# A tuned attention-plus-feed-forward kernel: query weights loaded through transposing DMAs, key-value sums formed the other way round, and all steps in a new order

## The chip, the cores and the metric

The kernel runs on one core of one Trainium2 chip. The metric is the device time of one execution in microseconds (us); lower is better. Five engines work side by side: PE (TensorE, matmuls), DVE (VectorE), ACT (ScalarE), POOL (GpSimd) and SP (SyncE, which here only issues DMAs). Each takes its own instructions strictly in order. They wait for one another through semaphores.

## The reference

The input x has 2048 tokens of 448 features. It is normalised per token, and two branches are computed from the same normalised x and added to x: a linear attention with 16 heads of 28 features, and a feed-forward block of width 1792 with the mish activation. All inputs and the output are bf16.

```python
xn = _layernorm(x)
qkv = (xn @ wqkv)                                  # 448 -> 3 x 16 heads x 28
pq = einsum("bhsd,hdf->bhsf", q, w_phi);  pk = einsum("bhsd,hdf->bhsf", k, w_phi)
phi_q = concatenate([softmax(pq), softmax(-pq)]);  phi_k = concatenate([softmax(pk), softmax(-pk)])
kv = einsum("bhsf,bhsd->bhfd", phi_k, v);          z = sum over s of phi_k
o = einsum("bhqf,bhfd->bhqd", phi_q, kv) / (einsum("bhqf,bhf->bhq", phi_q, z) + 1e-6)
h = xn @ w1 + b1
out = x + o @ wo + (h * tanh(softplus(h))) @ w2
```

## The kernel before

The 2048 tokens are 16 tiles of 128, taken in 8 pairs u = 0 to 7. Everything stays in on-chip memory: x, both weight sets, the activations. The program is a list of named steps, `ORDER`, written out as text. Each name calls a function that records instructions for the engines; a small recorder (`Program`) notes which instruction reads and writes what and puts in the semaphore waits. So the order of the names sets the order of every engine's queue at once, and an instruction that must wait holds up all that stands behind it on its engine. SP's queue holds nearly all DMAs, loads and turns alike; the bias (`lba`) and W2 (`l2a`) are issued by ACT.

The steps, with the letters used in the order:

- `lx..`, `lkm`, `lqm`, `lvm`, `lkt`, `lqt`, `lp`, `l1m`, `l1t`, `l2`, `lo`: loads of x (in parts), of the key, query and value weights (rows 0 to 383, and the last 64 rows twice as a tail), of w_phi, W1, W2 and Wo. The last letter is the issuing engine (s is SP, a is ACT).
- `st`, `rs`, `xn`, `xt`: layernorm statistics of a pair (DVE), reciprocal deviation (ACT or POOL), the normalised pair (DVE or POOL), and its transpose into `xnT`, either by PE with a copy (letters a, d) or by one DMA (m, line 465).
- `wtk`, `wtq` and `wmk`, `wmq`: w_phi is folded into the key and query weights. The weights are transposed on PE (`w_tr`, line 493), copied out, and multiplied with a block-diagonal w_phi (`w_mm`, line 506). This gives `Wpk` and `Wpq`. Query weights so take 16 transposes and two copies.
- `kUF`, `kUH`, `vUF`, `vUH`, `qQ.GF`, `qQ.GH`, `fQ.CF`, `fQ.CH`: products with xnT, all at line 393 (`pair_part`). F is the part over three full blocks of 128 rows, six matmuls for two tiles; H is the rest of 64 rows, two matmuls, one in each half of the array. When both parts are done ACT applies exp (k, q) or mish (f), or ACT or DVE copies (v). q and f work on 1024 tokens at a time (half Q = 0 or 1), f on one of 14 blocks C of the hidden width.
- `knU.S`: k's softmax. DVE sums the exponentials and takes the reciprocal, POOL multiplies (line 551).
- `kvU`: the sums over tokens of phi_k times [v, 1], accumulated in one bank (line 570). Per pair 32 matmuls: for each sign s, tile, head group g and half r, a stationary 128x56 block of phi_k and 58 moving columns of v. The two halves r write different partitions.
- `kvz`: DVE masks the sums into `KVZ`, with the epsilon (lines 582 and 587).
- `ndT`: numerator and denominator of a tile T: 16 matmuls of 60 columns (line 641), then seven DVE instructions. The result goes through a DMA transpose (`otUm`, line 676) to `wo`.
- `gT`, `woUF`, `woUH`: second feed-forward product (14 matmuls, line 710) and output projection (line 725), accumulated in one bank per tile. After the third part DVE adds x, and `sto` or `stt` stores.
- `zN`: N warm-up matmuls on zeros. `b1` turns the bias. `pi`, `pm`, `pw`, `pk`, `pv`: masks, identity, zeros and ones made on POOL. `table` loads ACT's exp table.

PSUM has eight banks, which the recorder hands out in pairs to open products. A step that needs a pair waits until the engine that empties it is done.

Of the kernel before, what the change touches and what calls it, by code (L numbers as in the profile page):

```python
# [12 lines left out]
D = 448  # L13
# [15 lines left out]
KVW = 2 * (DH + 1)  # L29
# [119 lines left out]
pk lx1s lba zero pm lx2s st1 z12 pw lkms pi table st3 rs3a rs1p b1 lps xn1d bd wtk0a xn3p lkts lqms st2 z2 xt1a wtk1d  # L149
lqts wmk0a rs2p wtq0d wtq1d wmk1a pv xt3d wmq0a lx4s xn2p wmq1a lvms st7 st4 rs4p rs7a xn7d k1F k3F xn4p st5 lx0s st6  # L150
k1H rs5p v1Hd xt2m xt7m k3H v3Ha v1Fa v3Fa rs6a xn5d k2F v2Fd xn6p k2H v7Hd v2Ha xt4m xt5m k7H v7Fa k7F st0 rs0a v4Fa
kn1.1 k4F xt6m kn3.1 k5H v4Ha kn3.0 k4H v5Hd k5F xn0d v6Fa kn7.1 xt0m v5Fa q1.2F q1.2H kn2.0 kn5.0 k0H q1.1H v6Hd
kn2.1 k0F q1.1F v0Fa kn5.1 kn7.0 kn4.0 k6F k6H q0.1H v0Hd q1.3H q0.1F q1.3F q0.0F q1.0F kn4.1 q0.2H q1.0H l1ts kn6.0
kn6.1 q0.0H kv4 l1ms kv5 kv7 kv2 q0.2F los q0.3F f0.1F kn0.1 f1.8H q0.3H kn1.0 f0.1H kv1 kv3 kv6 kn0.0 kv0 f1.8F kvz
f1.10F f1.1F f1.5H f1.1H nd2 f1.10H f1.5F f0.0F f0.2H f1.11H f0.0H nd0 f0.2F f1.11F f1.7F f0.13F f1.7H f0.13H nd1
f1.13H f1.13F f1.9F f0.6F ot0m f0.6H nd3 f1.9H f0.8H f0.8F f0.5F f0.9F f0.5H f0.7H f0.9H nd4 f0.7F f1.2F nd5 ot1m
f1.12H f0.10H f1.2H l2a f0.10F f1.12F f1.3F f1.6H f0.12H f1.3H nd6 f1.6F f0.12F f0.11F f1.4H nd7 f0.4H f0.11H f0.4F
f1.4F f0.3F ot3m nd10 nd11 f0.3H ot2m f1.0H f1.0F wo3F g6 wo0F wo3H ot5m wo0H nd8 nd9 g1 g0 g7 wo5F nd14 ot4m nd12
wo2H wo5H g4 wo1F g5 g11 g10 wo2F wo4F nd13 wo1H wo4H sto3 nd15 ot6m g3 sto2 ot7m g9 g12 g2 wo6H wo7H g15 sto5 sto0
g8 g13 wo6F sto4 wo7F stt15 g14 sto1 sto6 stt14  # L160
# [8 lines left out]
def _kernel(es, nc, A_x, A_wqkv, A_w_phi, A_wo, B_w1, B_b1, B_w2, out):  # L169
# [10 lines left out]
    mask2 = sb("mask2", [P, 2], FP32)  # L180
# [18 lines left out]
    Wq = sb("Wq", [P, 4, D], BF16)  # L199
    Wqk = [Wq, Wk]  # L200
    Wp = [sb("Wpq", [P, 4, G * P], BF16), sb("Wpk", [P, 4, D], BF16)]
    WT = [[sb(f"WT{w}{i}", [GP, 2, G, P], BF16) for i in range(2)] for w in range(2)]
    actT = sb("actT", [P, FC, S], BF16)
    zeros = actT[:, 0, 0:TCW]
    Sk = [sb(f"Sk{i}", [P, 2, 2 * H], FP32) for i in range(NU)]
    rSk = [sb(f"rSk{i}", [P, 2, 2 * H], FP32) for i in range(NU)]
    v_flat = sb("v_all", [P, NU * 2 * H * (DH + 1)], BF16)
    v_all = v_flat[:, :].rearrange("p (u i h c) -> p u i h c", u=NU, i=2, h=H)
    EqT = sb("EqT", [P, 2, G, S], BF16)
    KVZ = sb("KVZ", [P, 2, G, 2, DH + 2], BF16)  # L210
# [15 lines left out]
    oT_home = [(Wkv, 0, ["Wk", "Wv"]), (Wkv, 14 * P, []), (Wq, 0, ["Wq"]), (Wp[1], 0, ["Wp1"])]  # L226
    home_rows = {"Wk": [("Wk", 0), ("Wt", 0), ("Wt", 1)], "Wv": [("Wv", 0)], "Wq": [("Wq", i) for i in range(3)],
# [65 lines left out]

    def p_ident():
# [19 lines left out]
    def p_ones():  # L314
        op("POOL", lambda e: e.memset(v_all[:, :, :, :, DH:DH + 1], 1.0), w=[("v1",)], tag="pv0")

    def p_mask2():
        op("POOL", lambda e: e.memset(mask2[:], 1.0), w=[("mask2",)], tag="pk0")
        for r in range(2):
            lo, hi = HALF[r]  # L320
            op("POOL", lambda e, lo=lo, hi=hi: e.affine_select(
                out=mask2[lo:hi], in_=mask2[lo:hi], compare_op=ALU.is_ge, fill=0.0, base=0, channel_multiplier=1,
                pattern=[[-DH, 2]]), r=[("mask2",)], w=[("mask2",)], tag="pk1")
            op("POOL", lambda e, lo=lo, hi=hi: e.affine_select(
                out=mask2[lo:hi], in_=mask2[lo:hi], compare_op=ALU.is_ge, fill=0.0, base=DH - 1, channel_multiplier=-1,
                pattern=[[DH, 2]]), r=[("mask2",)], w=[("mask2",)], tag="pk2")
        op("POOL", lambda e: e.tensor_copy(ap_on(KVZ[:, 0, 0, 0, DH + 1:DH + 2], [[NDW, 2 * G], [DH + 2, 2]]),
                                           ap_on(mask2[:, 0:1], [[0, 2 * G], [1, 2]])), r=[("mask2",)], w=[("KVZ1",)],
           tag="pk3")

    def zero():
        op("DVE", lambda e: e.memset(zeros.bitcast(mybir.dt.uint32), 0), w=[("zeros",)], tag="zeros")

    def warm(n):
        b = take1()

        def f(e):
            for _ in range(n):
                ins = e.matmul(bank(b)[:, :], zeros[:, 0:P], zeros[:, :], start=True, stop=True)
            return ins  # L340
        pe(f, [("zeros",)], [pb(b)], f"warm{n}")
# [142 lines left out]
    def w_tr(which, h, eng):  # L484
# [5 lines left out]
        def tr(e):  # L490
            for c in range(2):
                for g in range(G):
                    ins = e.transpose(oT()[:, c, g, :], Wqk[which][:, 2 * h + c, g * GP:(g + 1) * GP], ident[:])
            return ins
        pe(tr, rows_of("Wq" if which == 0 else "Wk")[:1 + 2 * h] + [("ident",)], [pb(b)], f"wtr{which}{h}")
        evac(eng, lambda: WT[which][h][:, :, :, :].rearrange("p c g n -> p (c g n)"),
             lambda: oT().rearrange("p c g n -> p (c g n)"), [pb(b)], [("WT", which, h)], f"wtre{which}{h}")

    def w_mm(which, h, eng):
        b = take2(False)  # L500
        n = (P, GP)[which]

        def mm(e):
            for c in range(2):
                for g in range(G):
                    ins = e.matmul(bank(b + c)[:, g * n:(g + 1) * n], WT[which][h][:, c, g, :], Wbd[:, g, :, 0:n // 2],
                                   start=True, stop=True)
            return ins
        pe(mm, [("WT", which, h), ("Wbd", 0), ("Wbd", 1)], [pb(b), pb(b + 1)], f"wmm{which}{h}")
# [47 lines left out]
    def kv_mm(u):  # L557
# [6 lines left out]
        def f(e):  # L564
            for s in range(2):
                for par in range(2):
                    for g in range(G):
                        for r in range(2):
                            at = (s * G + g) * KVW
                            ins = e.matmul(bank(kvb)[64 * r:64 * r + QP, at:at + KVW],  # L570
                                           E_of(u)[:, s, par, (4 * r + g) * QP:(4 * r + g + 1) * QP],
                                           v_all[:, u, par, 8 * r + 2 * g:8 * r + 2 * g + 2, :],
                                           start=(first and s == 0 and par == 0 and g == 0), stop=(last and par == 1),
                                           skip_group_check=True)
# [3 lines left out]
    def kvz():  # L578
        kvb = kv_bank[0]
        for r in range(2):  # L580
            lo, hi = 64 * r, 64 * r + QP
            op("DVE", lambda e, r=r, lo=lo, hi=hi: e.tensor_tensor(
                ap_on(KVZ[lo:hi, 0, 0, 0, 0:1], [[NDW, 2 * G], [DH + 2, 2], [1, DH]]),
                ap_on(bank(kvb)[lo:hi, 0:1], [[KVW, 2 * G], [DH + 1, 2], [1, DH]]),
                ap_on(mask2[lo:hi, 0:1], [[0, 2 * G], [1, 2], [0, DH]]), ALU.mult),
               r=[pb(kvb), ("mask2",)], w=[("KVZ", r)], tag=f"kvz{r}")
            op("DVE", lambda e, r=r, lo=lo, hi=hi: e.scalar_tensor_tensor(
                ap_on(KVZ[lo:hi, 0, 0, 0, DH:DH + 1], [[NDW, 2 * G], [DH + 2, 2]]),
                ap_on(bank(kvb)[lo:hi, DH:DH + 1], [[KVW, 2 * G], [DH + 1, 2]]), DEN_EPS / 2,
                ap_on(mask2[lo:hi, 0:1], [[0, 2 * G], [1, 2]]), ALU.add, ALU.mult),  # L590
               r=[pb(kvb), ("mask2",)], w=[("KVZz", r)], tag=f"kvzz{r}")
        free2(kvb)

# [39 lines left out]
    def nd(t):  # L633
        b = take2(False)

        def f(e):
            for s in range(2):
                for g in range(G):
                    for r in range(2):
                        at = (s * G + g) * NDW  # L640
                        ins = e.matmul(bank(b + r)[:, at:at + NDW], EqT[64 * r:64 * r + QP, s, g, tok(t)],  # L641
                                       KVZ[64 * r:64 * r + QP, s, g, :, :], start=True, stop=True)
            return ins
        pe(f, [("Eq", s, g, t // 8) for s in range(2) for g in range(G)]
           + [(n, r) for n in ("KVZ", "KVZz") for r in range(2)] + [("KVZ1",)], [pb(b), pb(b + 1)], f"nd{t}")
# [119 lines left out]
    for which, n in ((0, "q"), (1, "k")):  # L765
        for h in range(2):
            for eng, c in (("ACT", "a"), ("DVE", "d")):
                add(f"wt{n}{h}{c}", w_tr, which, h, eng)
# [10 lines left out]
    for eng, c in (("SP", "s"), ("ACT", "a")):  # L779
        for name, a, b in (("x0", 0, 2), ("x1", 2, 4), ("x2", 4, 8), ("x4", 8, 16)):  # L780
            add(f"l{name}{c}", load_x, a, b, eng)
        for i, (n, t) in enumerate((("q", Wq), ("k", Wk), ("v", Wv))):
            add(f"l{n}m{c}", load_main, eng, "W" + n, t, A_wqkv[:, i * D:(i + 1) * D])
        add(f"lqt{c}", load_tail, eng, "Wq", Wq, A_wqkv[:, 0:D])
# [3 lines left out]
        for name, fn in (("p", load_phi), ("b", load_b1), ("2", load_w2), ("o", load_wo)):  # L788
            add(f"l{name}{c}", fn, eng)
    add("b1", bias_T)  # L790
    for n, fn in (("pi", p_ident), ("pm", p_mask), ("pw", p_wbd), ("pv", p_ones), ("pk", p_mask2), ("zero", zero)):
        add(n, fn)
# [55 lines left out]
```

## Time and profile before

| what | value |
|---|---|
| median of 3 runs | 158.92 us (157.85 to 158.98) |
| profiled execution | 159.08 us, of which the span of instructions is 157.3 |
| PE busy, share of the span | 150.2 us, 95% |
| DVE | 100.6 us, 64% |
| ACT | 73.4 us, 47% |
| POOL | 42.0 us, 27% |
| moved by DMA | 12.72 MB |
| granted TensorE clock | 1.00 |

The span runs from the first to the last instruction, and the execution's own time is 1.8 us longer. In the profile a line such as "PE PS L393 MATMUL" names the engine, what it writes and the line of the kernel. PEld is the load of a matmul's stationary operand; it overlaps with PE. Rows of a timeline give start and duration in us; because matmuls are pipelined, each one's duration includes its latency, and the start of the next row tells when its columns had gone in. Waits are listed as who waited for whom: total us, times, longest. SPq is SP's issuing of a DMA; "us to landing" counts from the start of that.

### The profile page before, as it was taken

How to read it: one execution, taken by the hardware profiler on the slowest of the kernel's cores; microseconds unless marked ns; L12 is line 12 of the kernel's file. 1: busy time of each engine (PE TensorE's matmuls, PEld its weight loads, DVE VectorE, ACT ScalarE, POOL GpSimd, SP SyncE). 2: the span in 40 equal slices, each digit the busy share in tenths (PEclk: the TensorE clock that was granted, in tenths of full speed). 3: DMA queues.
4: the chain of work that ended last, by engine and by line, in shares of the span. 5: the costliest groups of instructions: out<-in, count | busy, mean ns of one | idle time of the engine just before them, and what ended most of it. 6: DMA issues, size and time to landing. Idle time of an engine off the chain costs nothing.

```text
span 157.3 us, 3093 instructions
## 1 busy us (share of the span) xinstructions
PE 150.2 (95%) x1309; PEld 74.1 (47%) x1309; DVE 100.6 (64%) x220; ACT 73.4 (47%) x84; POOL 42.0 (27%) x57
## 2 busy tenths in 40 slices
PE   6699999969999999999999999999999999999992
PEld 2394444424464644444444444555455555545550
DVE  2995899999994217745486665969686159710141
ACT  3286989969989768765578566300000000000000
POOL 6494767599999400000000000000000000000000
PEclk9999999999999999999999999999999999999999
DMA  4994353199400000003216604230310000940104
GB/s 155 284 329 107 71 105 70 23 212 367 130 10 0 4 0 4 0 0 58 41 21 194 214 4 79 38 63 2 58 58 4 0 0 0 154 142 0 58 26 149
DMA packets 20217, 12.72 MB, mean 81 GB/s; under 512 B 13932, under 2 KB 19436, under 8 KB 20204
## 3 DMA queue, kind: packets, MB, share of 16 engines
q1 hardware_dynamic: 18368, 10.92, 27.7%
q10 hardware_dynamic: 1836, 1.61, 3.4%
q8 instruction: 10, 0.16, 0.5%
q14 instruction: 3, 0.02, 0.1%
HBM read 7.48 MB, written 1.84 MB: 59 GB/s over the span
## 4 chain that ended last, share of the span: by engine, by line
PE 77%; DVE 10%; DMA 7%; SPq 3%; issue 1%; POOL 1%; DVEq 0%
PE PS L393 38%; PE PS L710 27%; PE PS L725 7%; DMA x_all<-in_A_x_dram 5%; DVE stats L412 3%; PE PS L641 3%; PE PS L570 2%; DVE xn L446 2%; DVE Sk L547 2%; DMA xnT<-xn 2%; SPq L265 1%; DVE mv L414 1%; SPq L260 1%; SPq L257 1%; DVE rSk L549 0%
## 5 line engine op out<-in xcount | busy, mean ns | idle before, releaser
L393 PE MATMUL PS<-xnT,W 128*128 128x512 bf16 (+1 forms) x224 | 45.8, 379 | 0.0
L710 PE MATMUL PS<-W,actT 128*128 128x448 bf16 x224 | 43.6, 353 | 0.0
L619 ACT ACTIVATE actT<-PS,b1T 128x1024 bf16<-128x1024 f32 x28 | 30.3, 1112 | 14.6 <-PE PS L393 14.6
L710 PEld LDWEIGHTS PS<-W,actT 128*128 128x128 bf16 x224 | 21.6, 98 | 20.6 <-issue 0.7
L393 PEld LDWEIGHTS PS<-xnT,W 128*128 128x128 bf16 (+1 forms) x224 | 17.6, 97 | 23.8 <-issue 4.3
L551 POOL TENSOR_TENSOR actT<-actT,rSk 128x896 bf16<-128x896 bf16 x16 | 26.6, 1697 | 2.9 <-DVE rSk L549 2.9
L700 DVE TENSOR_TENSOR x_all<-PS,x_all 128x448 bf16<-128x448 f32 x16 | 9.6, 621 | 22.9 <-PE PS L710 18.1
L547 DVE TENSOR_REDUCE Sk<-actT 128x32 f32<-128x896 bf16 x16 | 16.6, 1038 | 0.0
L605 ACT ACTIVATE EqT<-PS 128x1024 bf16<-128x1024 f32 x16 | 15.2, 1033 | 2.3 <-PE PS L393 2.3
L657 DVE COPY Sq<-PS 128x16 f32<-128x16 f32 x32 | 4.1, 168 | 17.7 <-PE PS L641 17.7
L539 ACT ACTIVATE actT<-PS 128x896 bf16<-128x896 f32 x16 | 13.6, 919 | 1.7 <-PE PS L393 1.3
L393 PE MATMUL PS<-Wpk,xnT 128*128 128x448 bf16 (+1 forms) x64 | 12.9, 354 | 1.3 <-DMA xnT<-xn 1.3
L393 PE MATMUL PS<-xnT,Wpq 128*128 128x512 bf16 (+1 forms) x64 | 13.6, 379 | 0.0
L393 PE MATMUL PS<-Wkv,xnT 128*128 128x448 bf16 (+1 forms) x64 | 12.7, 353 | 0.2 <-ACT actT L539 0.2
L412 DVE BATCH_NORM_STATS2 stats<-x_all 128x6 f32<-128x448 bf16 x16 | 9.7, 605 | 3.8 <-DMA x_all<-in_A_x_dram 3.8
L665 DVE TENSOR_TENSOR v_all<-v_all 128x464 f32<-128x464 f32 x16 | 10.3, 642 | 0.6
L661 DVE TENSOR_TENSOR v_all<-PS,Sq 128x464 f32<-128x464 f32 x16 | 10.3, 642 | 0.5
L668 DVE TENSOR_TENSOR xn<-v_all,rden 128x448 bf16<-128x448 f32 x16 | 10.0, 625 | 0.5
L663 DVE TENSOR_TENSOR v_all<-PS,Sq 128x464 f32<-128x464 f32 x16 | 10.1, 630 | 0.0
L393 PEld LDWEIGHTS PS<-Wpk,xnT 128*128 128x128 bf16 (+1 forms) x64 | 5.3, 96 | 7.6 <-issue 3.6
L393 PEld LDWEIGHTS PS<-xnT,Wpq 128*128 128x128 bf16 (+1 forms) x64 | 5.2, 97 | 6.6 <-issue 0.8
L393 PEld LDWEIGHTS PS<-Wkv,xnT 128*128 128x128 bf16 (+1 forms) x64 | 5.2, 97 | 6.0 <-ACT actT L539 1.0
(64 smaller groups left out, 111.5 us busy)
## 6 DMA issues: line engine op xcount, KB each, us to landing
W<-in_B_w_dram ACTq DMA_DIRECT2D x1, 1568.0 KB, 7.0
out_dram<-x_all SPq DMA_DIRECT2D x7, 224.0 KB, 2.2
W<-in_B_w_dram SPq DMA_DIRECT2D x1, 1344.0 KB, 9.9
x_all<-in_A_x_dram SPq DMA_DIRECT2D x1, 896.0 KB, 7.5
Wkv<-in_A_wqkv_dram SPq DMA_DIRECT2D x2, 336.0 KB, 6.4
Wo<-in_A_wo_dram SPq DMA_DIRECT2D x2, 336.0 KB, 10.4
x_all<-in_A_x_dram SPq DMA_DIRECT2D x2, 224.0 KB, 5.2
x_all<-in_A_x_dram SPq DMA_DIRECT2D x1, 448.0 KB, 3.6
```

Of the source, the lines that this page charges most:

```text
L393: ins = e.matmul(o, lhs(c, k), rhs(c, k), start=first and c in (0, 3), stop=not first and c in (2, 3))
L412: op("DVE", lambda e, t=t: e.bn_stats(stats[:, t, :], x_all[:, t, :]), r=[("x", t)], w=[("st", t)], tag=f"bn{t}")
L539: op("ACT", lambda e, s=s: e.activation(E_of(u)[:, s, :, :], two(b, D), ACT.Exp, scale=1.0 if s == 0 else -1.0), r=[pb(b), pb(b + 1)], w=[ ...
L547: op("DVE", lambda e: e.tensor_reduce(Sk[u][:, s, :], Eh(), AX.X, ALU.add), r=[("E", u, s)], w=[("Sk", u, s)], tag=f"Sk{u}.{s}")
L551: op("POOL", lambda e: e.tensor_tensor(Eh(), Eh(), ap_on(rSk[u][:, s, 0:1], [[1, 2 * H], [0, DH]]), ALU.mult), r=[("E", u, s), ("rSk", u, ...
L605: op("ACT", lambda e, s=s: e.activation(EqT[:, s, g, q * 1024:(q + 1) * 1024], bank(b, 2), ACT.Exp, scale=1.0 if s == 0 else -1.0), r=[pb( ...
L619: op("ACT", lambda e: e.activation(actT[:, fc, q * 1024:(q + 1) * 1024], bank(b, 2), ACT.Mish, bias=b1T[:, fc:fc + 1]), r=[("b1T",), pb(b) ...
L661: op("DVE", lambda e: e.tensor_tensor(tv(t1[i]), num(0), sx(1), ALU.mult), r=[pb(b), pb(b + 1), ("Sq", i, 1)], w=[("t1", i)], tag=f"ta{t}")
L663: op("DVE", lambda e: e.tensor_tensor(tv(t2), num(1), sx(0), ALU.mult), r=[pb(b), pb(b + 1), ("Sq", i, 0)], w=[("t2",)], tag=f"tb{t}")
L665: op("DVE", lambda e: e.tensor_tensor(t1[i], t1[i], t2, ALU.add), r=[("t1", i), ("t2",)], w=[("t1", i)], tag=f"tc{t}")
L710: ins = e.matmul(bank(b)[:, 0:D], actT[:, fc, tok(t)], W2[:, fc, :], start=first and fc == 0, stop=last and fc == FC - 1)
L725: ins = e.matmul(bank(b)[:, 0:D], oT_of(u)[lo:hi, cc * P:(cc + 1) * P], Wo[lo:hi, cc, :], start=first and c in (0, 3), stop=last and c in ...
```

## The change

Three things are changed, and several small ones with them.

1. *Query weights.* The plain loads of the query weights (`lqm`, `lqt`) and their PE transposes (`wtq`) are gone. Four transposing DMAs, `lqT0` to `lqT3`, load a block of four heads each (112 columns, read as 128, by 448 rows) straight into `WqT`, turned. A DVE copy (`qd`) doubles the last 64 columns, which the folding product then reads.
2. *Key-value sums.* v is now stationary (60 columns: two heads of 28, the one, and a spare) and phi_k moves, both signs at once: 16 matmuls of 112 columns per pair instead of 32 of 58. Half r still writes its own partitions. The sums arrive transposed. `kvz` masks them in two DVE instructions into `KVT`, and one DMA transpose from SP turns this into `KVZ`. v's rows are 30 wide instead of 29; the ones are set two at a time.
3. *Order.* All steps stand in a new order. The bias (`lbs`) and W2 (`l2s`) are issued by SP. `table` comes first. `pk` moves from the start of POOL's queue to after `rs6p`; `pv` lies between the sixth and seventh product of POOL. Seven f steps, with their mish, come before the last three q steps. All kv steps stand in one row.

Warm-ups read a 2-column zero tile with step 0 instead of a part of `actT`, set by POOL instead of DVE. Three small DVE instructions (`ep`) prepare the epsilon per row.

```diff
+    def load_qT(g, eng):
+        dma(eng, lambda e: e.dma_start_transpose(WqT[:, g, 0:D], A_wqkv[:, g * GP:g * GP + P]), w=[("WqT", g)],
+            tag=f"ldWqT{g}")
+    def double_qT():
+        op("DVE", lambda e: e.tensor_copy(WqT[:, :, D:4 * P], WqT[:, :, D - 64:D]), r=[("WqT", g) for g in range(G)],
+           w=[("WqTd",)], tag="qd")
...
+        def lhs(c, g):
+            if which:
+                return WT[h][:, c, g, :]
+            return WqT[0:GP, g, (2 * h + c) * P:(2 * h + c + 1) * P]
...
-            for s in range(2):
-                for par in range(2):
-                    for g in range(G):
-                        for r in range(2):
-                            at = (s * G + g) * KVW
-                            ins = e.matmul(bank(kvb)[64 * r:64 * r + QP, at:at + KVW],
-                                           E_of(u)[:, s, par, (4 * r + g) * QP:(4 * r + g + 1) * QP],
-                                           v_all[:, u, par, 8 * r + 2 * g:8 * r + 2 * g + 2, :],
...
+            for par in range(2):
+                for g in range(G):
+                    for r in range(2):
+                        ins = e.matmul(bank(kvb)[64 * r:64 * r + NDW, g * 2 * QP:(g + 1) * 2 * QP],
+                                       v_all[:, u, par, 8 * r + 2 * g:8 * r + 2 * g + 2, :],
+                                       E_of(u)[:, :, par, (4 * r + g) * QP:(4 * r + g + 1) * QP],
...
+        dma("SP", lambda e: e.dma_start_transpose(KVZ[:, :, :], KVT[:, :, :, :, :].rearrange("p g s x f -> p (g s x f)")),
+            r=[("KVT", 0), ("KVT", 1)], w=[("KVZ",)], tag="kvT")
...
-                                       KVZ[64 * r:64 * r + QP, s, g, :, :], start=True, stop=True)
+                                       KVZ[64 * r:64 * r + QP, 2 * g + s, 64 * r:64 * r + NDW], start=True, stop=True)
```

The new order up to the first nd step, which is where the prediction reckons:

```diff
+table zero lx1s pi lx2s st1 rs1a lbs z12 st3 b1 pm z1 lkms lkts pw xn1d wtk0a lps bd lvms z1 wtk1a lx4s lx0s z1 st2
+rs2p rs3a xt1d z1 z1 wmk0a lqT2 wmk1a lqT1 xn3d v1Fa xn2d lqT3 st4 xt3a k1H v1Ha rs4p st7 k1F v3Fd xt2m k3F xn4d rs7a
+lqT0 v3Ha qd v2Hd k3H k2H xt4m xn7p st0 v2Fa rs0a wmq1d k2F xt7m xn0d wmq0d k4F v4Fd k4H st5 v4Ha v7Ha rs5p xt0m l1ts
+k7H st6 k7F v7Fd rs6p xn5d q0.0F q0.0H v0Ha q0.1H pk k0H k0F xn6p xt5m kn7.0 kn3.1 q0.1F v0Fa xt6m k5F kn0.0 kn1.1
+kn4.0 q0.3F q0.3H k5H v6Hd l1ms q1.3H v6Fd q1.3F kn2.0 v5Fa k6F v5Ha k6H pv f1.5H q1.1H q1.1F f1.5F f0.1F kn5.0 kn5.1
+f1.2F f0.0F ep f1.4H kn4.1 f0.0H kn1.0 kn2.1 f0.1H f1.2H f1.4F f0.4F l2s kn6.1 f0.5F f0.4H q1.0H f0.5H q1.2H q1.2F
+kn6.0 q1.0F kn3.0 kn0.1 q0.2F kv4 kv5 los kv0 kv6 kv3 kv2 kv1 kn7.1 kv7 f0.2H q0.2H f0.11H kvz f0.11F f0.2F f0.8F
+f1.11F f1.11H f1.1H nd2 f0.8H f1.1F f0.13F nd3 f0.13H f1.6H nd1 f1.6F ot1m f0.7F f0.12F f0.12H f0.7H f1.0H nd6 f1.0F
...
+wo6F wo1F g3 wo7F g2 sto1 g9 g8 g12 sto4 stt15 g14 sto6 stt14
```

More of the change, by code (lines that the diff above doesn't have):

```diff
@@ L290, in table, with p_zero @@
            tag="table")
+    def p_zero():
+        op("POOL", lambda e: e.memset(zeros[:], 0.0), w=[("zeros",)], tag="zeros")
     def p_ident():
@@ L482, in w_bd, with w_tr @@
                r=[("Wraw",), ("mask",), ("Wbd0",)], w=[("Wbd", r)], tag=f"Wbd{r}")
-    def w_tr(which, h, eng):
+    def w_tr(h, eng):
         b = take1()
@@ L764, in _kernel @@
         add(f"stt{t}", store, t, t + 1)
[L765 to L768, printed above, removed]
+    for h in range(2):
+        for eng, c in (("ACT", "a"), ("DVE", "d")):
+            add(f"wtk{h}{c}", w_tr, h, eng)
+            for which, n in ((0, "q"), (1, "k")):
                 add(f"wm{n}{h}{c}", w_mm, which, h, eng)
```

105 lines of the change are left out of this document (50 added, 55 removed).

## The prediction

> **What bounds the kernel now.** I read the busy line and the slices of the page first.
>
> ```profile
> PE 150.2 (95%) x1309; PEld 74.1 (47%) x1309; DVE 100.6 (64%) x220; ACT 73.4 (47%) x84; POOL 42.0 (27%) x57
> ...
> PE   6699999969999999999999999999999999999992
> ```
>
> TensorE is busy nearly everywhere at a full clock, so the time is its work plus the few places where it waits. The first slices and the ninth (31 to 35 us) are the only thin ones. The waits, of which only those of PE count here, say why:
>
> ```profile
> PE PS L493 <- DMA Wkv<-in_A_wqkv_dram: 1.3, 1, 1.3
> PE PS L393 <- DMA xnT<-xn: 1.3, 1, 1.3
> ...
> PE PS L339 <- DVE actT L332: 1.2, 1, 1.2
> ```
>
> PE cannot begin before the key weights have landed, and it stops once for a turned pair of x tiles. The timeline of PE from 6.5 us gives the line that I reckon on:
>
> ```profile
> 6.79 0.66 PE L493 MATMUL PS<-ident,Wkv 128*112 128x128 bf16 x8 [1.29 <-DMA Wkv<-in_A_wqkv_dram]
> 7.28 0.60 PE L339 MATMUL PS<-actT 128*128 128x512 bf16 x2
> ...
> 8.65 0.55 PE L506 MATMUL PS<-Wbd,WT 112*128 112x112 bf16 x8
> 9.04 1.11 PE L493 MATMUL PS<-ident,Wq 128*112 128x128 bf16 x16
> 9.99 0.56 PE L506 MATMUL PS<-Wbd,WT 112*128 112x112 bf16 x8
> ```
>
> Starts are to be read as a chain: each row begins where the columns of the row before end. From 6.79 to the last matmul's end (its closing addition starts at 154.21) are 147.2 us without PE's last latency of 0.2. Of them about 2.0 are waits: the pair of half steps at 31.23 has 0.22 of columns and the next row starts at 32.88, so 1.4; k2F (17.18, six of 0.189: the chain has 14 such in 2.65) ends at 18.31 and v2F starts at 18.70, so 0.4; some 0.2 are small. What follows the last matmul (closing addition, last store) is 3.3 to the span's end of 157.3 and 1.8 more to the profiled time of 159.08. The new order ends with the same steps, so I leave these 5.1 as they are. The median of the three runs, 158.92, is 0.1% below the profiled one.
>
> **The change, part by part.** (a) *Start.* The bias load moves from ACT's queue to SP's, ahead of the key weights: one issue of 0.5. The key weights' issue ended at 2.15 and they landed just before 6.79, behind 672 KB of x of which the second part was first used at 4.90; so they are held by bytes more than by the issue. Between 0 and +0.5, I take +0.1.
>
> (b) *Query transposes leave PE.* Sixteen run from 8.99 to 9.93 in weight loads: -0.95. Two of the DVE copies of 0.67 go too, off PE's line.
>
> (c) *Key-value sums.* Now 32 matmuls of 58 columns for each pair; 128 of them take this long on the chain:
>
> ```profile
> 45.42 1.96 PE PS L570 x128
> ```
>
> That is 0.46 per pair of tiles without the switch, 14.4 ns for a matmul of 58 columns, which at the 0.42 ns per column of the warm-ups above (two of 512 from 7.28 to 7.71) would take 24; so the two column halves run side by side. After, 16 matmuls of 112 columns go as 8 such pairs; eight of 112 columns are the row at 8.65, 0.39 until the next starts. So 8 x 0.07 = -0.53. If the halves did not overlap it were 8 x 0.33 = +2.6; the row above excludes it, so I keep -0.6 to 0. The sums run once in a row of eight instead of twice in rows of four, and each change between full and half array costs about 0.1: 41 changes against 42, -0.1.
>
> (d) *Warm-ups.* After the first key transposes stand four single warm-up matmuls where there was one double: two more of 0.216, +0.43. They lie in waits for ACT's copies only in part; I count them whole.
>
> (e) *Old waits* go with the old order: -2.0. The 1.4 came from the pair xn0, whose DVE pieces stood against POOL's long products:
>
> ```profile
> L446 DVE TENSOR_SCALAR xn<-x_all,mv,rstd 128x64 bf16<-128x64 bf16 x4 | 2.6, 640 | 0.0
> ...
> L446 DVE TENSOR_SCALAR xn<-x_all,mv,rstd 128x384 bf16<-128x384 bf16 x4 | 1.5, 374 | 0.0
> ```
>
> A sixth of the columns took longer on average: one of these was held while POOL normalised. In the new order the last of these pieces precedes POOL's first product.
>
> (f) *New waits.* SP's queue now holds x1, x2, bias, keys, tails, phi, values, x4, x0, then three transposing query loads, the DMA turn of xn2, the fourth query load. Loads are served at 241 KB/us (x4 landed at 13.26; it and all before it except x1, first used at 3.39, are 2376 KB).
>
> ```profile
> 5.76 7.50 DMA x_all<-in_A_x_dram
> ...
> 29.85 2.90 DMA xnT<-xn
> ```
>
> Without the 448 KB of the old query loads x0 lands at 3.4 + 2492/241 = 13.7. A transposing load from HBM is not in this trace. The nearest row is the turn of a pair, 224 KB: 2.90, of which 1.22 is its issue. A quarter of the query weights is 112 KB, so at most 0.84 by that row and at least 0.46 at the plain rate; I take 0.7, nearer to the row that turns. Three: 15.8. The turn of xn2, issued at about 12, comes behind them and lands 1.4 later, at 17.2. PE needs it at v2H: 6.9, 2.9 of transposes, warm-ups and key products, 0.2 of wait for the tails, v1F 1.14, xT3 0.4, a wait of 0.1 for ACT's copy, three full steps 3.4, three half steps 0.6 and three changes 0.3 make 15.9. So the wait is 1.3 by these and 0.6 with the loads at the plain rate; and a transfer need not wait until the one before has reported its landing. I take 0.8. With the 0.3 for tails and ACT before it: +1.1. From 0, if x0 comes early, to 7.9, if each load took the row's 2.90 whole.
>
> The Trainium skill, page DMA: Bandwidth & Descriptors, section Latency and other measured facts, gives a transposing DMA 261 GB/s where the middle dimension isn't contiguous; by that a quarter would take 0.44 and the wait would nearly vanish (156.4). No run here shows it for HBM; the turn's 224 KB in 1.68 after its issue is slower, so the sum goes by that row.
>
> (g) *The doubled tail.* A DVE copy waits for the fourth query load and holds, behind it, the stats of x0 and POOL's xn7, hence xT7. The load lands 0.8 after the turn, the copy takes about 0.3; PE has half steps, v2F and a switch, 1.9, before the query product. Hidden with 0.6 to spare; what is later costs PE its full excess.
>
> (h) *The turn of the sums.* After the eight sums DVE does two products (0.62 each, like the two of now), then a DMA of eight blocks, 2.9 by seven; 4.6 in all with 0.2 from PE. Before nd2 PE has four full feed-forward steps of 1.3, five half steps and switches: 6.5. Hidden by 1.9. POOL's 16 products (1.66 apart) and a memset of 1.2, from about 30 us, end near 58, and the last sum starts near 60.
>
> (i) *W1.* Its main load is queued behind the turn of xn6, which waits for POOL (about 30 us), so issued near 31.2. PE reaches f1.5H 23.8 after v2H, at 40.6 (12 full steps of 1.14, four of 1.3, 17 half steps, two query products of 0.45, switches).
>
> ```profile
> W<-in_B_w_dram SPq DMA_DIRECT2D x1, 1344.0 KB, 9.9
> ```
>
> 9.9 after that is 41.1, but there 448 KB of tails stood just before it, 1.9 at 241; they now leave 8 us earlier. Between 0 and +0.6, I take +0.1.
>
> (j) *ACT tables.* Seven feed-forward steps precede the last three query steps: two more loads, 1.28 each by this row, and no PE wait, since four pairs of banks stand between.
>
> ```profile
> 53.91 1.28 ACT L619 ACT_TABLE_LOAD   x1
> ```
>
> The Trainium skill, page ScalarE: Activation LUTs, section What ACT_TABLE_LOAD costs, counts 2.66 for a switch, with a drain; the section Table sets asks for all of one set before switching, which the new order breaks. Here the function before ends at 53.89 and the next starts at 55.20, 1.31 in all, so the row disagrees with the larger figure.
>
> Sum: 0.1 - 0.95 - 0.53 - 0.1 + 0.43 - 2.0 + 1.1 + 0.1 = -1.85. 159.08 - 1.85 = 157.2.
>
> **Rivals.** (1) *The transposing loads are slow.* Each takes 2.1, three times my value (the far end above is beyond it). Then xT2 is 4.2 later, PE stops at v2H, and the copy in (g) is late by another 0.3: 157.2 + 4.5 = 161.7. Slower than before by over 1% from 1.8 each on. For it: three stand in one queue ahead of what PE needs next, and rows of 256 bytes lie 2688 apart in HBM. Against: turning costs little in SBUF. (2) *W1 late.* f1.5H waits 1.2 because W2 and Wo follow directly and the engines of a load end unevenly: 158.4. For: 9.9 against 7.0 for the larger W2. Against: the tails are gone from its front. (3) *The turn of xn2 arrives in time:* 156.4. (4) *ACT is the bound at the switches.* If a switch held ACT 1.3 longer than the row, f1.4H, f0.11H and nd2, which need banks, would wait about 1.1, 0.3 and 0.5: 159.1. Against: the row. By that page's 2.66 this is what would come.
>
> **How the numbers follow.** My forecast 0.45 (156.6 to 157.9, a quarter of it above 157.3), slow loads 0.21, W1 late 0.14, in time 0.12, ACT 0.08. About 1% (1.6 us) is what a measurement of this kernel tells from no change. Faster: 0.33 + 0.12 = 0.45; same: 0.12 + 0.14 + 0.08 = 0.34; slower 0.21. The range goes from 155.9 (no wait at v2H, tails in time, key weights not later) to 161.7 (slow loads); the forecast alone 156.6 to 157.9.
>
> **What would show it.** Right: PE waits about 0.8 at the first half step after the turn of xn2 and nowhere over 0.5 after 20 us; 128 sum matmuls take about 3.2 in one run; the last feed-forward matmuls end near 152. Wrong: a wait of PE for xnT over 2, for W near 40, or for KVZ before nd2; more table time than 2.6; or transposing loads that take over 1.8 each.

## The result, and the profile after

The kernel after takes 156.72 us (median of 6 runs, 155.76 to 157.51), the kernel before 158.09 in the same comparison (157.79 to 158.98); the ratio is 0.9897 with a 95% interval of 0.9853 to 0.9942. A second set of runs of the same kernel (below) gives 156.63 and 0.9877 (0.985 to 0.9904). So it is faster by 1.0 to 1.2%, and 0.5 us below the forecast of 157.2, inside its range (156.6 to 157.9) near the lower end. The profiled execution took 156.64 us with a span of 154.6; against the 159.08 and 157.3 of before that is 2.4 to 2.7 less.

Busy line and slices of the kernel after:

```profile
PE 150.3 (97%) x1168; PEld 72.6 (47%) x1168; DVE 101.3 (65%) x226; ACT 74.7 (48%) x83; POOL 38.6 (25%) x52
...
PE   7999999999999999999999999999999999999992
```

PE has 141 matmuls fewer and the same busy time. The lines of both kernels say why: the query transposes (1.1 us busy before) are gone and the sums are busy for 3.3 instead of 4.1, but the warm-ups are busy for 7.2 instead of 4.7, and these lie in waits. So the busy time does not show the gain. What is to be seen is in the slices: the thin ninth slice of before is full, and so are the second and those after it. Its waits are now these (who <- for whom: total, times, longest):

```profile
PE PS L355 <- POOL mhalf L306: 1.0, 1, 1.0
...
PE PS L410 <- DMA xnT<-xn: 0.3, 1, 0.3
PE PS L528 <- DVE WqT L273: 0.3, 1, 0.3
```

The first lies at the start, where PE waits for data anyway. The third has a cause on another engine: DVE's copy that doubles the tail stood waiting for the last transposing load, and that is the only place in the kernel where it waits so for a load of weights:

```profile
DVE WqT L273 <- DMA WqT<-in_A_wqkv_dram: 2.3, 1, 2.3
```

The chain of waits, in order of time (start, length, what), says what that cost:

```profile
11.54 0.64 DVE stats L429
12.18 0.64 SPq L482
...
12.86 4.75 DMA WqT<-in_A_wqkv_dram
...
18.05 1.75 POOL xn L458 x3
...
19.81 3.23 DMA xnT<-xn
...
23.18 34.38 PE PS L410 x182
57.56 3.27 PE PS L590 x128
```

The fourth query load is 4.75 us on its way, POOL's pair xn7 starts after the copy, its turn after that, and only from 23.18 on does PE run by itself, to the end without another wait. The timeline of PE around these places:

```profile
6.76 0.65 PE L510 MATMUL PS<-ident,Wkv 128*112 128x128 bf16 x8
...
15.47 0.55 PE L410 MATMUL PS<-Wkv,xnT 64*128 64x448 bf16 x4
...
16.33 1.31 PE L410 MATMUL PS<-Wkv,xnT 128*128 128x448 bf16 x6
17.92 0.62 PE L528 MATMUL PS<-Wbd,WqT 112*128 112x128 bf16 x8 [0.28 <-DVE WqT L273]
...
22.53 0.35 PE L410 MATMUL PS<-Wkv,xnT 64*128 64x448 bf16 x2
23.18 0.36 PE L410 MATMUL PS<-Wkv,xnT 64*128 64x448 bf16 x2 [0.29 <-DMA xnT<-xn]
```

By starts: six full matmuls take 1.14 elsewhere, and from 16.33 the next row comes after 1.59, so 0.45 are lost; two half matmuls take 0.19, and from 22.53 it is 0.65, again 0.45. At 15.47 four half matmuls follow each other (v3H, v2H): no wait there, where the prediction had 0.8.

From the first key transposes to the end of the last matmul by the trace it is 6.79 to 154.17 before and 6.76 to 151.83 after: 147.4 and 145.1, 2.3 less. What lies ahead of that stretch and behind it, to the execution's own time, is 0.1 less in all.

### The profile page after: what moved, and what is told of

Read it like the earlier page. It is cut to its first block, busy times and chain, and to the rows that moved or that the text cites. A ratio compares the mean times of both kernels' runs of the same rounds, so it can differ in the third digit from the quotient of the medians.

```text
span 154.6 us, 2812 instructions
## 1 busy us (share of the span) xinstructions
PE 150.3 (97%) x1168; PEld 72.6 (47%) x1168; DVE 101.3 (65%) x226; ACT 74.7 (48%) x83; POOL 38.6 (25%) x52
## 4 chain that ended last, share of the span: by engine, by line
PE 87%; DMA 5%; DVE 2%; ACT 2%; POOL 1%; issue 0%; SPq 0%; POOLq 0%
PE PS L410 44%; PE PS L727 28%; PE PS L742 7%; PE PS L355 4%; DMA WqT<-in_A_wqkv_dram 3%; PE PS L658 3%; PE PS L590 2%; DMA xnT<-xn 2%; ACT WT L475 1%; POOL xn L458 1%; DVE xn L463 1%; DVE stats L429 0%; SPq L482 0%; DVE x_all L717 0%; PE PS L510 0%
## 5 line engine op out<-in xcount | busy, mean ns | idle before, releaser
L410 PE MATMUL PS<-xnT,Wpq 128*128 128x512 bf16 (+1 forms) x64 | 14.1, 379 | 0.0
L355 PE MATMUL PS<-zeros 128*128 128x512 bf16 x17 | 7.2, 569 | 1.0 <-POOL mhalf L306 1.0
```

The costliest lines, as they stand in the source:

```text
L355: ins = e.matmul(bank(b)[:, :], ap_on(zeros[:, 0:1], [[0, P]]), ap_on(zeros[:, 0:1], [[0, TCW]]), start=True, stop=True)
L410: ins = e.matmul(o, lhs(c, k), rhs(c, k), start=first and c in (0, 3), stop=not first and c in (2, 3))
```

## The experiments

Of every run the traces give, for each transfer, when it was issued and when the first and the last of its 16 engines reported it landed. Landing times below that are not in a fence come from there. A *packet* below is one of 16 KB on the DMA queue that the page calls "instruction".

**The two kernels once more.** No edit.

> The kernel before once more, for a second profile. Theory: the first profile of before was one of its long executions (159.08 beside a median of 158.06), with its largest x load late; a second one then shows the x load near 12 instead of 13.3 us, PE's waits after 7 us near 1.0 instead of 2.0, and a time of about 158.0. Rival: the waits of 2.0 are in every execution: 159.0 again, with the same 1.3 for xnT.

> The changed kernel once more, on the chip where its variants run. Theory: 156.6 to 156.8 again, and again the transposing DMA in flight at 14 to 16 us lands late on one DMA engine, next to a packet of 16 KB on the instruction queue: the fourth query load lands 4.5 or more after its issue. Rival: that was one execution's chance, and it lands about 3 after its issue.

Before: 157.96 us, span 156.2, 1.1 below the first profile. Almost all of the difference is one wait. In the first profile of before x4 landed at 13.26 and DVE stood 1.62 for it; here it landed at 12.02. DVE's rows, first profile, then this one:

```profile
13.29 0.63 DVE L412 BATCH_NORM_STATS2 stats<-x_all 128x6 f32<-128x448 bf16 x1 [1.62 <-DMA x_all<-in_A_x_dram]
```

```profile
12.04 0.63 DVE L412 BATCH_NORM_STATS2 stats<-x_all 128x6 f32<-128x448 bf16 x1
```

The 1.2 us are carried along DVE's queue to the pair xn0 (its pieces begin at 26.06 instead of 27.18), and PE's row there starts at 31.77 instead of 32.88, with a wait of 0.3 instead of 1.3:

```profile
31.77 0.36 PE L393 MATMUL PS<-Wpk,xnT 64*128 64x448 bf16 x2 [0.30 <-DMA xnT<-xn]
```

So a part of the "old waits" of 2.0 is not the kernel's but that execution's; why x4 landed late there is open. The 25 runs of before beside the first four experiments spread from 157.6 to 159.6. After was stable: 156.63 (156.31 to 157.25), and again the fourth query load landed late, at 17.35.

**The fourth query load ahead of the turn of xn2.**

```diff
-... xn2d lqT3 st4 xt3a ... xt2m k3F xn4d rs7a lqT0 v3Ha qd v2Hd ...
+... xn2d lqT3 lqT0 st4 xt3a ... xt2m k3F xn4d rs7a v3Ha qd v2Hd ...
```

> The changed kernel with one DMA moved: the fourth transposing query load is issued right behind the third, ahead of the turn of xn2. Theory: the fourth load came late (landed near 17.6 us, 4.7 after its issue) only because of where it stood; DVE held 2.3 us for it, and PE waited 0.45 before the query product and 0.45 at v7H, whose x pair was delayed by the held DVE. Then DVE's wait for WqT falls under 0.5, both PE waits go, and the time is about 0.8 below the changed kernel: 155.9. Rival: something else in the first 20 us is late at that time whatever stands there (the turn of xn2 or of xn4 takes the hit): 156.7 or more, with a new wait of PE for xnT.

155.76 us, ratio 0.9843 (0.9808 to 0.9879), the lowest median of all runs. The load landed at 13.87 and DVE no longer waits for it. But in the profiled execution (156.44, one of the two longer of six; the other four took 155.62 to 155.83) another transfer is late in its place, the turn of xn2: issued at 11.67, first engine 14.44, last 16.32, so 4.6 where the kernel after has 3.0, and the half step of tile 2 waits 0.6 for it:

```profile
16.37 0.36 PE L410 MATMUL PS<-Wkv,xnT 64*128 64x448 bf16 x2 [0.43 <-DMA xnT<-xn]
```

So it is not only the fourth load that can be late at that time. What makes a transfer late, the last experiments ask.

**The fourth load first, and no single warm-ups.** As the last, without the five `z1`.

> The fourth query load right behind the third, and the five single warm-up matmuls left out (the twelve at the start stay). Theory: the warm-ups lie in waits for the folded w_phi and for ACT's copies, so leaving them out changes nothing: 155.8, as with the fourth load moved alone. Rival one: they are on PE's line, as the prediction counted them: 0.4 to 0.9 less, 155.1. Rival two: without them PE loses its full clock for a while at the start: 156.5 or more, with a longer time for the first matmuls.

155.83 us, ratio 0.9835 (0.9804 to 0.9866): no different from 155.76. These intervals alone could hide 0.4, but the trace shows it too: the warm-ups cost next to nothing, where the prediction had 0.43. They stand in gaps that are there without them: from the first key transposes to the key products it is 2.21 us here (6.71 to 8.92) and 2.29 in the kernel after (6.76 to 9.05), because POOL's `Wbd` is awaited either way. In this trace nothing lands late among the transposing transfers (the four loads 13.50, 13.91, 14.50 and 14.94, the turn 15.60), and neither the query product (17.81) nor v7H waits.

**Plain query loads and PE transposes.** The kernel after, with part 1 of the change undone.

```diff
-... lqT2 wmk1a lqT1 xn3d v1Fa xn2d lqT3 st4 ... lqT0 v3Ha qd v2Hd ... rs0a wmq1d
+... lqms wmk1a lqts xn3d v1Fa xn2d st4 ... v3Ha v2Hd ... rs0a wtq1d wtq0d wmq1d
```

> The changed kernel with the query weights as before: three plain loads in the place of the transposing ones, 16 PE transposes and two DVE copies ahead of the query product, the rest of the order kept. Theory: the transposes lie on PE's line, +0.94; DVE no longer waits for a fourth load, so up to 0.9 of PE waits go, but the two copies of 0.6 on DVE take some back: between 156.7 and 157.6, with 157.1 as the middle. Rival one: the transposes lie in waits and cost nothing: 155.8. Rival two: their copies on DVE delay what stands behind them and PE waits over 1 there: 158 or more.

157.51 us, ratio 0.9937 (0.9914 to 0.9961), 0.8 above after. The transposes are back on PE's line, and a wait for the copies with them:

```profile
17.72 1.06 PE L503 MATMUL PS<-ident,Wq 128*112 128x128 bf16 x16
19.12 0.62 PE L516 MATMUL PS<-Wbd,WT 112*128 112x128 bf16 x8 [0.34 <-DVE WT L470]
```

1.40 us from row to row: 0.95 of columns, as predicted, and 0.45 of wait. After has 0.45 there too (for the late load) and another 0.45 at v7H, so from these places part 1 is worth 0.5, and would be worth 1.4 without the late load. Another 0.25 stands ahead of them: v2F starts at 16.58 here and at 16.33 in after. Together these are the 0.8 of the medians.

**Key-value sums as before.** The kernel after, with part 2 undone.

> The changed kernel with the key-value sums as before: 32 matmuls of 58 columns for each pair, the masked sums written by DVE straight into KVZ, no DMA turn. Theory: eight times 0.46 instead of 0.39, so the run of sums takes 3.7 instead of 3.15 and the time is 0.5 to 0.6 longer: 157.3. Rival: the turn by DMA costs PE something before nd2 that now goes; then the time is the same or shorter, 156.7 or less.

157.47 us, ratio 0.9936 (0.9908 to 0.9963), 0.75 above after. The sums in this kernel, then in the kernel after:

```profile
57.13 3.91 PE L584 MATMUL PS<-v_all,actT 128*56 128x58 bf16 x256
60.97 0.39 PE L402 MATMUL PS<-xnT,W 64*128 64x512 bf16 x2
```

```profile
57.49 3.34 PE L590 MATMUL PS<-actT,v_all 128*60 128x112 bf16 x128
60.76 0.39 PE L410 MATMUL PS<-xnT,W 64*128 64x512 bf16 x2
```

3.84 us against 3.27 by starts: 0.57 for eight pairs. The other 0.2 of the medians is not accounted for.

**Before, with xn0 normalised earlier.** The kernel before; the pair xn0 moved ahead on DVE, to where POOL has no product yet, and its rstd to POOL.

```diff
-... k7H v7Fa k7F st0 rs0a v4Fa kn1.1 ... k5F xn0d v6Fa kn7.1 xt0m v5Fa ...
+... k7H v7Fa k7F st0 rs0p xn0d xt0m v4Fa kn1.1 ... k5F v6Fa kn7.1 v5Fa ...
```

> The kernel before with one step moved: pair 0 is normalised (deviation on POOL, pieces on DVE) ahead of the first k softmax, so none of its DVE pieces runs beside POOL's long products. Theory: DVE's pieces were held by POOL (1.67 us for 64 columns), that made the turn of xn0 late, and PE waited 1.4 for it; then the pieces take 0.3 to 0.4 each, PE's wait for xnT goes and the time falls by 1.2 to 1.5 from before's 158.1, to about 156.8. Rival: the wait only moves (the sums wait for POOL, which starts its products about 2 us later): 157.8 to 158.3.

158.21 us, ratio 1.0005 (0.9979 to 1.003): nothing. The first half of the theory held: the pieces of 64 columns take 354 ns on average instead of 640, and PE's wait for xnT is gone. But another one came. First the group (busy us in all, mean ns), then PE's timeline:

```profile
L446 DVE TENSOR_SCALAR xn<-x_all,mv,rstd 128x64 bf16<-128x64 bf16 x4 | 1.4, 354 | 0.0
```

```profile
26.13 1.31 PE L393 MATMUL PS<-Wpk,xnT 128*128 128x448 bf16 x6
28.47 1.86 PE L393 MATMUL PS<-Wkv,xnT 128*128 128x448 bf16 x9 [1.03 <-ACT actT L539]
```

PE gets to v6F sooner than ACT has emptied a pair of banks: 2.34 from row to row where 1.14 are columns. One step moved does not pay; the wait goes to the next engine.

**The new order alone.** Both part 1 and part 2 undone, the order kept.

> The new order without the two other parts: query weights loaded plain and turned on PE, sums of 32 matmuls per pair and no turn of them. Theory: the two parts are worth 0.8 and 0.7 by their undoing one at a time, they lie in different stretches and add up, so the order alone is at 158.2, the same as before. Rival: the order itself gains what before's waits cost, about 1: 157.2, and the two parts overlap.

159.1 us, ratio 1.0039 (1.0019 to 1.0059): slower than before. With 0.8 for the query loads and 0.75 for the sums on top of 156.7 it should have been 158.2. The missing 0.9 stands in one place, behind the sums:

```profile
57.81 3.87 PE L572 MATMUL PS<-v_all,actT 128*56 128x58 bf16 x256
61.61 0.39 PE L395 MATMUL PS<-xnT,W 64*128 64x512 bf16 x1
62.96 0.37 PE L395 MATMUL PS<-xnT,W 64*128 64x512 bf16 x1 [0.96 <-issue]
```

The second matmul of one half step comes 1.35 behind the first, where the two start within 0.01 of each other in the same step of other runs, and "issue" says that the profile shows nothing that held it. The sums are 256 matmuls with 256 weight loads in 3.8 us. The DMA records show ten packets; PE's 2647 matmuls and weight loads come to one for about every 256 of them (in after 2358 and nine packets). One packet here began at 60.33, took 1.41 us and ended at 61.74; PE stood until 62.96. So PE may have run out of instructions. Against it: the run *Key-value sums as before* has the same row of 256 in 3.84 us with a packet at its end (60.37 to 61.30), and its half steps follow without a stop.

**The new order alone, with the sums in two rows of four.** Two full feed-forward steps between them.

```diff
-kn6.0 q1.0F kn3.0 kn0.1 q0.2F kv4 kv5 los kv0 kv6 kv3 kv2 kv1 kn7.1 kv7 f0.2H q0.2H f0.11H kvz f0.11F f0.2F f0.8F
+kn6.0 q1.0F kn3.0 kn0.1 q0.2F kv4 kv5 los kv0 kv6 f0.11F f0.2F kv3 kv2 kv1 kn7.1 kv7 f0.2H q0.2H f0.11H kvz f0.8F
```

> The new order alone (as in e6_order_alone), with the eight key-value sums in two runs of four, two full feature steps (f0.11F and f0.2F) between them. In e6_order_alone TensorE stood still for 1.13 us behind the sums (f0.2H to q0.2H 1.35 us in place of 0.22) on no semaphore, and the instruction packet of 60.33 us took 1.41 us and ended at 61.74; 512 instructions of the sums are used up in 3.7 us there. Theory: TensorE ran out of instructions; with 2.6 us of slow matmuls between the two runs the fetch comes in time, the standstill is gone, two more switches between whole and split matmuls cost 0.2, and the time is 159.1 - 1.1 + 0.2 = 158.2. Rival: the standstill is a wait for a bank or for ScalarE that no record names; then it is found again at the half steps behind the last sums and the time is 159.1 or more.

The standstill is gone, as the theory had it, but the time is 161.97 us, ratio 1.0227 (1.0157 to 1.0298), 3.8 above what it expected:

```profile
62.99 2.03 PE L572 MATMUL PS<-v_all,actT 128*56 128x58 bf16 x128
64.95 0.39 PE L395 MATMUL PS<-xnT,W 64*128 64x512 bf16 x2
65.17 0.38 PE L395 MATMUL PS<-xnT,Wpq 64*128 64x512 bf16 x2
65.39 0.38 PE L395 MATMUL PS<-xnT,W 64*128 64x512 bf16 x2
66.55 1.47 PE L395 MATMUL PS<-xnT,W 128*128 128x512 bf16 x6 [0.78 <-ACT actT L621]
69.80 1.79 PE L395 MATMUL PS<-xnT,W 128*128 128x512 bf16 x8 [1.78 <-ACT EqT L607]
```

The half steps follow each other by 0.22. Then PE waits for banks: the three products whose halves stand behind the sums are complete within 0.7 of each other, and from 66.55 to 69.80 one step takes 3.25 instead of 1.30. The edit also changed ACT's work, which the expectation left out: the mish of f0.2 now comes ahead of the exp of q0.2, so ACT loads its table four times in this stretch (at 55.95, 61.03, 66.51 and 69.76) where the run before did it twice (55.42 and 65.54). The last two:

```profile
66.51 1.28 ACT L607 ACT_TABLE_LOAD   x1
...
69.76 1.28 ACT L621 ACT_TABLE_LOAD   x1
```

Two more loads are 2.6 us of ACT while PE waits for its banks. That PE ran short of instructions fits both traces, but the sums with part 2 alone undone ran without a standstill in one row, and no run supplied instructions sooner with all else kept; it is not shown. The repair cost more than the fault.

**After without the single warm-ups.** Only the five `z1` removed.

> The kernel after without the five single warm-up matmuls at the start, so that TensorE's instruction stream is ten instructions shorter ahead of every later step. In the traces so far a 16 KB instruction packet begins after some 180 to 205 TensorE instructions (at 15.61 us in the kernel after), holds one DMA engine for about 1 us, and the turn or transposing load that is moving just then lands about 1.7 us late: in the kernel after this was the fourth transposing load (17.6 us in place of 15.9). Theory: with the stream five matmuls shorter the packet begins about 1 us later, near 16.6 us, when no transposing transfer moves its data; the fourth load lands by 16.2, DVE's wait for it falls from 2.3 us to under 1, the 0.45 us wait of TensorE ahead of the queries' merged weights and the 0.45 at v7H are gone, and the time is 155.8, as with the fourth load issued first. Rival: the load is late because it is issued last, behind the turn of xn2; then it lands near 17.6 again and the time stays at 156.6. A second rival, the prediction's own price of the warm-ups (0.43 us on the path): 156.2 with the load still late.

156.59 us, ratio 0.989 (0.9838 to 0.9942): as after, so again no price of warm-ups. As a test of the packet it failed: the packet began at 15.48, about where it does in after (15.61 and 15.22 in its two profiles), and the fourth load landed at 17.53. By the traces 181 matmuls and weight loads of PE had begun by then here, and 197 and 191 in after: the count at which a packet starts scatters by more than the ten instructions that were taken out. Neither theory is touched by that.

**The packet moved by more instructions.** The warm-up of 512 columns as two of 256: the same columns, twice the instructions; in the first of the two runs for the twelve at the start alone, in the second for the five single ones as well.

```diff
-            for _ in range(n):
-                ins = e.matmul(bank(b)[:, :], ap_on(zeros[:, 0:1], [[0, P]]), ap_on(zeros[:, 0:1], [[0, TCW]]), start=True,
+            for _ in range(2 * n):
+                w = TCW // 2
+                ins = e.matmul(bank(b)[:, 0:w], ap_on(zeros[:, 0:1], [[0, P]]), ap_on(zeros[:, 0:1], [[0, w]]), start=True,
```

> The kernel after with the twelve first warm-up matmuls of 512 columns cut into twenty-four of 256: the same columns at the same place, but 24 more instructions in TensorE's stream ahead of everything else. Theory: the 16 KB instruction packet goes with the count of TensorE's instructions, so it begins twelve matmuls earlier, near 13.2 us in place of 15.6; the fourth transposing load, unchanged in its place behind the turn of xn2, then lands by 16.2 in place of 17.6, DVE's wait for it falls from 2.3 us to under 1, and what moves at 13.2 to 14.2 (the third transposing load or the turn of xn2) is late instead, up to 1.7 us; time 155.8 to 156.4, by whether the half step of tile 2 then waits. Rival: the load is late because of its place; it lands near 17.6 wherever the packet falls, and the time stays at 156.6.

> As e9_halved_first_warm, with the five single warm-ups cut in two as well: 34 more instructions in all, seventeen matmuls. Theory: the packet begins near 12.3 us, when x4, x0 and the first transposing loads land; one of these is late by up to 1.7 us and those behind it on the same engine too, the fourth load lands by 16.2, and the time is 155.8 to 156.6. Rival: the fourth load lands near 17.6 and the time stays at 156.6.

The first packet began at 13.13 and at 12.33 us (expected 13.2 and 12.3), and the fourth load, at its old place, landed at 16.46 and 16.23 (expected by 16.2) instead of 17.61. In the first run another transfer that moves at the time of the packet is now late, the third load, whose first engine reported at 13.68 and whose last at 15.32. The DMA rows of the first run (KB are not given; us from issue to landing), for the third load and the fourth:

```profile
WqT<-in_A_wqkv_dram SPq DMA_TRANSPOSE x1, 6.2
...
WqT<-in_A_wqkv_dram SPq DMA_TRANSPOSE x1, 3.5
```

In the kernel after these are 4.8 and 4.8. DVE's wait is down from 2.3 to 0.8, and both stops of PE are gone:

```profile
DVE WqT L273 <- DMA WqT<-in_A_wqkv_dram: 0.8, 1, 0.8
```

So the rival, the load's place, falls: with a packet in it the fourth load landed at 17.34 to 17.61 (four traces with that place), with the packet moved at 16.46 and 16.23. But the second run did not do what was expected of it: its packet lay over the second and the third load, and neither was late. Together:

| kernel | packet, us | late transfer, first to last engine |
|---|---|---|
| after | 15.61 to 16.57 | fourth load, 15.90 to 17.61 |
| after again | 15.22 to 16.18 | fourth load, 15.53 to 17.35 |
| fourth load first | 14.34 to 15.30 | turn of xn2, 14.44 to 16.32 |
| fourth first, no warm-ups | 15.46 to 16.42 | none moving; turn of xn2 15.43 to 15.60 |
| first warm-ups halved | 13.13 to 14.30 | third load, 13.68 to 15.32 |
| all warm-ups halved | 12.33 to 13.48 | neither second (12.50 to 12.57) nor third load (12.87 to 13.15); turn of xn2 15.13 to 15.70 |

A packet does not always make a transfer late. The fourteen traces hold 196 turns of 224 KB (of x and of the output). For 24 of them a packet began 1.0 to 2.8 us after their issue: 11 took 4.4 to 4.7 us, one 3.7, and 12 took 2.9 to 3.0, as without a packet. Of the other 172 none took over 4.1, and 159 of them under 3.1. So a delay of over 1.2 us came only with a packet, but in half of the cases the packet did nothing.

The times are 156.41 us (0.9843, 0.9787 to 0.9898) and 156.34 (0.9845, 0.98 to 0.9891), 0.3 under after, which these intervals do not tell from nothing. In the profiles more was there: PE was 0.44 and 0.70 us ahead of the kernel after at 24 us. The next packet, moved as well, to 32.53 and 32.01, meets the turn of xn6. In the first run this takes 4.6 us where it took 2.9, and PE loses 0.36 of its lead:

```profile
34.14 0.35 PE L411 MATMUL PS<-Wpk,xnT 64*128 64x448 bf16 x2
34.69 0.36 PE L411 MATMUL PS<-Wkv,xnT 64*128 64x448 bf16 x2 [0.20 <-DMA xnT<-xn]
```

Open is why a packet of about 1 us can make a transposing transfer 1.4 to 1.9 us later, why it often does not, and why the turn of xn2 was late by about 0.7 on all engines in the second of these runs.

The fastest versions are those with the fourth load first: 155.83 us where after has 156.63 in the same comparison, 0.5% less, and 1.6% less than before.

## Why the prediction was right, and where not

(a) *Start.* +0.1 was taken; the first key transposes begin at 6.76 instead of 6.79. The issue of the bias cost nothing.

(b) *Query transposes.* -0.95 is right: the run with plain loads shows them with 0.95 of columns.

(c) *Sums.* Predicted -0.53 and -0.1 for switches. By starts the eight take 3.27 us, against twice 1.96 before, so -0.65. A pair takes 0.39 (128 matmuls start from 57.49 to 60.62, ahead of the last switch). The two column halves do run side by side with 112 columns too, as the key products had suggested.

```profile
L590 PE MATMUL PS<-actT,v_all 128*60 128x112 bf16 x128 | 3.3, 213 | 0.0
```

(d) *Warm-ups.* The size came out, the cause did not. From the first key transposes to the first key products it was 1.86 us before (6.79 to 8.65) and is 2.29 after (6.76 to 9.05): +0.43, to the digit. But in the two runs without the single warm-ups it is 2.21 and 2.28, so they lie in a wait, for POOL's `Wbd`. In the new order the load of w_phi stands behind the key tails; it landed at 7.71 instead of 7.00, and `Wbd` followed. A wait that the prediction did not have took the place of the cost that it had: luck.

(e) *Old waits.* Taken from one execution at 2.0. The second profile of before has 1.1 less, by one load that landed earlier. The sum was made against an execution of 159.08, and against that the gain was 2.4 where 1.85 was forecast; the usual gain, 1.4 to 2.0 by the medians, is smaller for this reason. The time that was forecast does not suffer from it, since the 1.1 stands both in the time that it starts from and in what (e) takes off. The mechanism of the 1.4 was half right: DVE's pieces were held by POOL's products (in after the pieces of 64 columns take 297 ns instead of 640, below), but with x4 in time little of the wait is left: in the second profile of before xn0's pieces are held as long, 2.65 us for the three, and PE waits 0.3 instead of 1.3. The other 1.0 came because DVE got to them late, after x4.

```profile
L463 DVE TENSOR_SCALAR xn<-x_all,mv,rstd 128x64 bf16<-128x64 bf16 x6 | 1.8, 297 | 0.0
```

(f) and (g) *New waits.* 1.1 was predicted, 0.8 of it at v2H for the turn of xn2, and the copy behind the fourth load "hidden with 0.6 to spare". At these places 0.9 came, and all of it from (g). Two steps failed, in opposite directions. x0 landed at 12.12, not 13.7, and the three loads followed at 12.66, 13.08 and 13.69: 0.54, 0.42 and 0.61 each, not 0.7. So the turn of xn2 landed at 14.53, 2.7 earlier than reckoned, before PE needed it at 15.67. That is rival 3, at its place; rival 1, 2.1 a load, is far off. The figure of the Trainium skill (page DMA: Bandwidth & Descriptors, section Latency and other measured facts), 261 GB/s, by which a quarter would take 0.44 (an estimate), is the nearer one; the trace agrees within 0.1 on average, though here the loads come from HBM. The choice of the higher value, by the row of a whole turn behind its issue, was wrong. But PE then reached the query product at 17.47, and the fourth load, with the packet in it, landed only at 17.61. The total of the waits was right by luck: two errors cancel.

(h) *Turn of the sums.* Predicted hidden by 1.9. DVE's two products take 0.68 each, the turn is issued at 62.28 and landed at 65.36, and nd2 starts at 67.24: 1.9 to spare.

```profile
L602 DVE SCALAR_TENSOR_TENSOR KVT<-PS,epsT,mask 60x448 bf16<-60x448 f32 x2 | 1.4, 683 | 7.3 <-PE PS L590 7.2
```

(i) *W1.* No wait: the load is issued at 31.64 and takes 6.6, and f1.5H starts at 40.46, predicted 40.6. Rival 2 is out.

```profile
W<-in_B_w_dram SPq DMA_DIRECT2D x1, 1344.0 KB, 6.6
```

(j) *Tables.* Two more loads, 1.28 each, no wait of PE behind them; rival 4 is out. The 2.66 of the Trainium skill (page ScalarE: Activation LUTs, section What ACT_TABLE_LOAD costs) is not seen here either: ACT's last mish ends at 55.09 and its next exp starts at 56.40, 1.31 in all.

```profile
L636 ACT ACT_TABLE_LOAD x2 | 2.6, 1283 | 0.0
...
L622 ACT ACT_TABLE_LOAD x1 | 1.3, 1283 | 0.0
```

The sum: the -2.3 between first transposes and last matmul are -0.95 (b), -0.65 (c), +0.43 at the start (the wait for `Wbd`), -2.0 old waits and +0.9 new ones, which is -2.27. Predicted were -0.95, -0.63, +0.43, -2.0 and +1.1; the +0.1 for W1 fell away. Of the three signs of being right two came, the sums in 3.27 us and the last feed-forward matmuls' end at 151.8, predicted near 152. The first, a wait of 0.8 behind the turn of xn2, did not.

## What to carry to other kernels

A wait that a single profile shows may belong to that execution: before a gain is booked for removing it, look whether the transfer behind it landed early or late, and take a second profile. When a reordering seems to be worth the waits it removes, ask which engine is next in line: moving one step (xn0) or two (the feed-forward steps between the sums) gave the wait to ACT's emptying of banks. The new order alone did not pay either; with one of the other parts it was 0.6% faster than before, with both 1.0 to 1.2%. When a term of a sum comes out to the digit, look still whether its cause did: here a wait for another load had taken its place. A transfer that PE needs soon is best issued with some 2 us to spare, since the packets of the program's own instructions can hold it up.

## What the runs showed of the hardware that was not expected

- PE's instructions arrive over the same DMA engines: packets of 16 KB, one for about 256 matmuls and weight loads, each 0.9 to 1.6 us on one engine. Of 24 turns in which such a packet began 1.0 to 2.8 us after their issue, 12 were 0.8 to 1.8 us late and 12 not at all. For the fourth query load, moving the packet by twelve matmuls took the delay away and gave it to the third.
- Behind a row of 256 matmuls with their weight loads in 3.8 us PE stood for 1.1 us with nothing in the profile that held it, in one kernel; in another the same row had no such standstill, and neither had two rows of 128. That the instructions came too late is likely and not shown. The 128 matmuls of part 2 show no standstill.
- A transposing load of 112 KB from HBM took 0.4 to 0.6 us behind another one, though its issue holds SP for 1.3 to 1.5 us.
